# Second MoE, round two: h w2 in seven products of quarters, weights kept in DRAM, outputs added by transfers

## The chip, the cores and the metric

One core of a Trainium2 chip. The metric is the device time of one execution in microseconds, lower is better; the times are those of whole executions, the trace is of one profiled execution.

## The reference

Attention in chunks, a gated MoE, and a second MoE; the change concerns the last.

```python
def _moe2_ref(x, domain_probs, w1, w2):      # x: 1536 tokens x 512
    p = domain_probs / (domain_probs.sum(-1, keepdims=True) + 1e-09)
    out = np.zeros((N, D), dtype=np.float32)
    for e in range(E):                        # 4 experts, 1024 features each
        h = np.maximum(x @ w1[e], 0.0)
        out += p[:, e:e + 1] * (h @ w2[e])
    return out
```

## The kernel before

Every float32 operand of a matmul is held as a high part (rounded to fp32r) and a low part (the rest), and one product is three matmuls: high by high, high by low, low by high (mm3, lines 176 to 179). All of TensorE's matmuls of the second MoE come from these three lines.

The order of instructions is written out by hand: each engine takes its instructions in the order in which the program emits them, and each waits for the buffers that it reads or overwrites. SyncE (SP) issues all transfers of the second MoE, in program order as well. A pool's tile waits until the readers of the tile before it in the same buffer are done.

The second MoE (second_block, line 359) runs in two rounds of 768 tokens, and each round in 8 blocks; a block is one expert's half of the features (512), as two groups of rows. Blocks are counted through: 0 to 7 in round one, 8 to 15 in round two.

The first layer of a block, x w1, is done by Winograd's form of Strassen's method: seven products of quarters for eight (tokens in halves of HT = 384, input features in halves, output features in halves). unit(n, u) (line 405) does them for one half u of the output columns: product(n, u, m) (line 375) is 6 matmuls of 384 columns into a PSUM tile b, e or a. In between, held (line 400, ScalarE) copies a partial sum out of PSUM, and the next product is added onto the same PSUM tile, so that product has to wait for the copy. total (line 395, VectorE) adds up, h_hi (line 387, ScalarE) and h_lo (line 390, VectorE) apply relu and split. In a block: products 1, 7, then the left-over of the block before (prev), products 6, 2, 4, 5, and product 3 later.

The second layer, h w2, is plain: o_part (line 443) does, for one tile of 128 tokens and one half u, 6 matmuls of 512 columns; 12 such parts make a block (72 matmuls), one of them being carried into the next block as prev. flush (line 452, VectorE) adds the scaled result into acc; in the last block of a round acc is sent out.

The weights of block n+1 are prepared while block n runs. w1_prep (line 236, 9 steps) makes the seven quarter sums of w1 and splits them: 7 casts on ScalarE, 7 subtractions and 4 sums on VectorE. w2_prep (line 272, 5 steps) splits w2: 4 casts, 4 subtractions. Raw weights come by raw1_to (4 buffers, two per group) and raw2_to (2 buffers, both of one group). The steps are put in a list, hooks; hook() takes one step off at a place in the matmul order: two places in each o_part, while at least two steps stay in the list, and the rest in the units of the next block. y_prep_late does the same for the tokens of round two. PSUM has 8 banks for these tiles, taken in turn.

Of the kernel before, what the change touches and what calls it, by code (L numbers as in the profile page):

```python
# [42 lines left out]
RT = 2 * HT // 128  # L43
NGR = 2
GW = FE // 2 // NGR

# [22 lines left out]
def fused_kernel(ctx: ExitStack, tc: tile.TileContext, kq0, kq1, kvw, kvc, vl, w_g, w_v, w_o, w_1, w_2, probs, out):  # L69
# [23 lines left out]
    def f32(ap):  # L93
        return ap.bitcast(F32)
# [98 lines left out]
    blocks = [(0, e, g) for e in range(NE) for g in range(NGR)]  # L193
    blocks += [(1, e, g) for e in reversed(range(NE)) for g in reversed(range(NGR))]

    groups = [b[1:] for b in blocks[:NE * NGR]] + [b[1:] for b in blocks[NE * NGR + 1:]]
    group_of = [n if n < NE * NGR else n - 1 for n in range(len(blocks))]
    yr, yops, raw1, raw2s = [], [], {}, {}
    ops1, ops2 = {}, {}
    pools = {}  # L200

    def raw1_to(n):
# [25 lines left out]
    def both(*parts):  # L228
        return lambda: [p() for p in parts]
# [6 lines left out]
    def w1_prep(n):  # L236

        t = {}

        def start():  # L240
            raw1_to(n + 1)
            r0, r1 = raw1[n]
            t.update(a11=r0[:, :2], a12=r0[:, 2:], a21=r1[:, :2], a22=r1[:, 2:])
            ops1[n] = {}

        def hi(m, a):
            def do():
                w = wp.tile([128, 2, 2, GW], F32R, tag="w", name=f"w1_{n}_{m}")
                ops1[n][m] = w
                nc.scalar.copy(out=w[:, 0], in_=t[a])  # L250
            return do

        def lo(m, a):
            def do():
                w = ops1[n][m]
                nc.vector.tensor_tensor(out=w[:, 1], in0=t[a], in1=f32(w[:, 0]), op=ALU.subtract)  # L256
            return do

        def comb(dst, a, b, op):
# [12 lines left out]
    def w2_prep(n):  # L272
        def hi(u, fh):
            def do():
                raw2_to(n + 1)
                w = pools["wp2"].tile([128, 2, DM], F32R, tag="w2", name=f"w2_{n}_{u}_{fh}")
                ops2[n, u, fh] = w
                nc.scalar.copy(out=w[:, 0], in_=raw2s[n][fh][:, u])  # L278
            return do

        def lo(u, fh):
            def do():
                w = ops2[n, u, fh]
                nc.vector.tensor_tensor(out=w[:, 1], in0=raw2s[n][fh][:, u], in1=f32(w[:, 0]), op=ALU.subtract)  # L284
                if (u, fh) == (1, 1):
                    raw2_to(n + 2)
            return do


        h, l = ([fn(u, fh) for u in range(2) for fh in range(2)] for fn in (hi, lo))  # L290
        return [both(h[0], h[1], l[0]), both(h[2], l[1]), l[2], h[3], l[3]]

    def y_ops():

# [60 lines left out]
    def emit(todo, n):  # L355
        for _ in range(min(n, len(todo))):
            todo.pop(0)()

    def second_block():
        sp = ctx.enter_context(tc.tile_pool(name="sp", bufs=1, reuse_waits="tile"))  # L360
        wp2 = pools["wp2"] = ctx.enter_context(tc.tile_pool(name="wp2", bufs=7, reuse_waits="tile"))
# [4 lines left out]
        H2, hooks = {}, []  # L366
        raw2_to(1)

        def hook(n=1, keep=0):
# [3 lines left out]
            return sp.tile([128, HT], F32, tag=name, bufs=n, name=name)  # L373

        def product(n, u, m, ps, first):
            w, y = ops1[group_of[n]][m], yops[0][m]
# [28 lines left out]
        def unit(n, u, prev):  # L405

            b, e = ps_tile(f"b{n}_{u}"), ps_tile(f"e{n}_{u}")
            product(n, u, 1, b, True)
            s1 = held(b)
            product(n, u, 7, e, True)  # L410
            s7 = held(e)
            a = None
            if prev is None:
                a = ps_tile(f"a{n}_{u}")
# [12 lines left out]
            c21 = total("v", e, s2)  # L427
            h_lo(n, u, (0, 0), c11)
            h_hi(n, u, (1, 0), c21)
            product(n, u, 5, b, False)  # L430
            c22 = total("v", b, s7)
            h_lo(n, u, (1, 0), c21)
            h_hi(n, u, (1, 1), c22)
            h_lo(n, u, (1, 1), c22)
            hook()

            def finish():
                product(n, u, 3, b, False)
# [4 lines left out]
        def o_part(n, d, tt, u, first, last, cols):  # L443
            th, c = divmod(tt, RT // 2)
            c = slice(c * 128, (c + 1) * 128)
            for fh in range(2):
                h, w = H2[n, u, (fh, th)], ops2[group_of[n], u, fh]
                mm3(d[:, cols], h[:, 0, c], h[:, 1, c], w[:, 0, cols], w[:, 1, cols],
                    first and fh == 0, last and fh == 1)
                hook(keep=2)  # L450

        def flush(n, d, tt, cols):
            j, e, g = blocks[n]
            i = n - j * NE * NGR
            p, a = p_sb[:, j * RT + tt, e:e + 1], acc[tt][:, cols]
            if i == 0:
# [3 lines left out]
            if i == NE * NGR - 1:  # L460
                t0 = (j * RT + tt) * 128
                nc.sync.dma_start(out=out[t0:t0 + 128, cols], in_=a)

        ALL = slice(0, DM)
        prev = None
        hooks.extend(w2_prep(0))
        for n in range(len(blocks)):
            end = n == len(blocks) - 1
            if n == 2:
                for do in y_sums(1, yr[0], nc.vector)[2].values():  # L470
                    do()
# [2 lines left out]
                hook(2)  # L474
            fin1 = unit(n, 1, fin0)
            hook(len(hooks))

            if n == NE * NGR - 1:
                hooks.extend(y_prep_late(1))
            elif not end:  # L480
                g = group_of[n + 1]
                hooks.extend(w1_prep(g) + w2_prep(g))
            ds, waiting = {}, []

            def part(tt, u, d_first=0, d_last=1):
                if tt not in ds:
# [18 lines left out]
            part(4, 0)  # L505
            flushed(3)
            part(4, 1)
            if not end:
                part(5, 0)
                flushed(4)  # L510

                def prev(n=n, ds=ds):
                    o_part(n, ds[5], 5, 1, False, True, ALL)
                    flush(n, ds[5], 5, ALL)
            else:
                flushed(4)
                for c0 in range(0, DM, DM // 2):
                    cols = slice(c0, c0 + DM // 2)
                    d = ps_tile(f"d{n}_5_{c0}")
                    for u in range(2):  # L520
                        o_part(n, d, 5, u, u == 0, u == 1, cols)
                    flush(n, d, 5, cols)
        pools["yo"].release()


# [430 lines left out]
```

## Time and profile before

| | us |
|---|---|
| median of 3 runs | 850.06 (849.72 to 851.29) |
| the profiled execution | 849.83 |
| its span, first to last instruction | 848.1 |
| round one, first matmul of block 0 to first of block 8 | 344.57 to 593.34 |
| round two, to the start of the last matmul | 593.34 to 844.63 |

PE is TensorE's matmuls, PEld its weight loads, DVE VectorE, ACT ScalarE, POOL GpSimd, SPq the queue of SyncE that issues transfers. A matmul's record is longer than the spacing to the next, since they overlap; spacing is read from the starts.

### The profile page before, as it was taken

Reading aid. Unit: us, or ns where it says so; the run is one execution under the profiler, and the core shown is the slowest. Engines: PE = TensorE matmul, PEld = TensorE weight load, DVE = VectorE, ACT = ScalarE, POOL = GpSimd, SP = SyncE. Lnnn points to the kernel's source line nnn. Section 1 sums busy time; section 2 is a strip of 40 time slices with the busy share of each in tenths; the row PEclk is TensorE's granted clock in tenths of the full one; section 3 lists DMA queues with packets and bytes.
Section 4 is the critical chain, followed back from the end, with each engine's and each line's share of the span. In section 5 each row is a group of like instructions: output and inputs, shape, how many; then the busy total and the mean of one; then the engine's idle time right before and its main releaser. Section 6 shows DMA issues by size and latency. Waiting matters only on the chain.

```text
span 848.1 us, 11989 instructions
## 1 busy us (share of the span) xinstructions
PE 841.7 (99%) x4826; PEld 744.0 (88%) x4826; DVE 485.4 (57%) x863; ACT 350.8 (41%) x726; POOL 19.9 (2%) x23
## 2 busy tenths in 40 slices
PE   9999999999999999999999999999999999999998
PEld 6899998888888888889988988988998998998997
DVE  7854346432342239468668567565667657657753
ACT  5765354332232345435334334433434533524520
POOL 2311000000000000000000000000000000000000
PEclk9999999999999999999999999999999999999999
DMA  8974134121120000322122122022022022020001
GB/s 305 370 277 160 28 124 147 50 73 40 63 75 1 1 0 18 131 77 65 59 75 91 34 75 99 26 75 75 26 76 99 26 84 91 26 100 25 26 1 75
DMA packets 18647, 69.23 MB, mean 82 GB/s; under 512 B 2320, under 2 KB 2592, under 8 KB 18592
## 3 DMA queue, kind: packets, MB, share of 16 engines
q1 hardware_dynamic: 18560, 68.45, 23.1%
q8 instruction: 38, 0.62, 0.3%
q14 instruction: 17, 0.14, 0.1%
q0 software_dynamic: 32, 0.02, 0.0%
HBM read 65.31 MB, written 3.15 MB: 81 GB/s over the span
## 4 chain that ended last, share of the span: by engine, by line
PE 97%; ACT 1%; DVE 1%; DMA 0%; POOL 0%; issue 0%; ACTq 0%; DVEq 0%
PE d L179 10%; PE d L178 10%; PE d L177 10%; PE b L178 5%; PE b L177 5%; PE b L179 5%; PE pv L177 4%; PE pv L179 4%; PE pv L178 4%; PE pg L177 4%; PE pb L179 4%; PE pb L177 4%; PE pg L178 4%; PE pg L179 4%; PE pb L178 4%; PE e L177 3%
## 5 line engine op out<-in xcount | busy, mean ns | idle before, releaser
L459 DVE SCALAR_TENSOR_TENSOR acc<-d,p_sb,acc 128x512 f32<-128x512 f32 (+1 forms) x85 | 59.9, 741 | 75.3 <-PE d L179 75.3
L402 ACT COPY s<-b 128x384 f32<-128x384 f32 x64 | 30.4, 475 | 169.5 <-PE b L179 169.5
L177 PE MATMUL b<-yo,w 128*128 128x384 f32 x256 | 86.5, 338 | 0.7 <-ACT s L402 0.7
L178 PE MATMUL b<-yo,w 128*128 128x384 f32 x256 | 86.5, 338 | 0.5 <-DVE yo L223 0.5
L179 PE MATMUL b<-yo,w 128*128 128x384 f32 x256 | 86.4, 337 | 0.0
L256 DVE TENSOR_TENSOR w<-raw,w 128x512 fp32r<-128x512 f32 x105 | 68.3, 685 | 0.0
L177 PE MATMUL pv<-xs,w_v 128*128 128x384 f32 (+1 forms) x176 | 64.2, 365 | 0.0
L250 ACT CAST w<-raw 128x512 fp32r<-128x512 f32 x105 | 60.5, 617 | 5.8 <-DVE raw L260 3.3
L179 PE MATMUL pv<-xs,w_v 128*128 128x384 f32 (+1 forms) x176 | 61.8, 351 | 0.3 <-POOL w_v L157 0.3
L178 PE MATMUL pv<-xs,w_v 128*128 128x384 f32 (+1 forms) x176 | 61.5, 349 | 0.0
L698 ACT ACTIVATE sg<-pg 128x512 f32<-128x512 f32 x36 | 21.5, 598 | 84.2 <-PE pg L179 84.2
L179 PE MATMUL pg<-xs,w_g 128*128 128x512 f32 x144 | 56.0, 389 | 0.0
L178 PE MATMUL pg<-xs,w_g 128*128 128x512 f32 x144 | 56.0, 389 | 0.0
L177 PE MATMUL pb<-hl,w_o 128*128 128x512 f32 x144 | 56.0, 389 | 0.0
L178 PE MATMUL pb<-hl,w_o 128*128 128x512 f32 x144 | 56.0, 389 | 0.0
L179 PE MATMUL pb<-hl,w_o 128*128 128x512 f32 x144 | 56.0, 389 | 0.0
L177 PE MATMUL pg<-xs,w_g 128*128 128x512 f32 x144 | 56.0, 389 | 0.0
L116 DVE TENSOR_TENSOR hl<-g,hl 128x512 fp32r<-128x512 f32 x36 | 24.7, 690 | 48.5 <-ACT hl L115 48.5
L177 PEld LDWEIGHTS b<-yo,w 128*128 128x128 f32 x256 | 48.1, 188 | 3.0 <-ACT s L402 1.0
L178 PEld LDWEIGHTS b<-yo,w 128*128 128x128 f32 x256 | 48.1, 188 | 2.8 <-DVE yo L223 0.8
L179 PEld LDWEIGHTS b<-yo,w 128*128 128x128 f32 x256 | 48.1, 188 | 0.0
L284 DVE TENSOR_TENSOR w<-raw,w 128x512 fp32r<-128x512 f32 x60 | 38.7, 685 | 12.5 <-ACT w L278 12.5
(1115 smaller groups left out, 1927.4 us busy)
## 6 DMA issues: line engine op xcount, KB each, us to landing
raw<-in_w_dram SPq DMA_DIRECT2D x60, 512.0 KB, 3.8
kv<-in_kvc_dram SPq DMA_DIRECT2D x20, 483.0 KB, 6.5
raw<-in_w_v_dram SPq DMA_DIRECT2D x12, 512.0 KB, 6.7
raw<-in_w_g_dram SPq DMA_DIRECT2D x12, 512.0 KB, 5.1
raw<-in_w_o_dram SPq DMA_DIRECT2D x12, 512.0 KB, 3.4
kv<-in_kvw_dram SPq DMA_DIRECT2D x8, 395.0 KB, 4.7
out_dram<-acc SPq DMA_DIRECT2D x11, 256.0 KB, 2.0
kv<-in_vl_dram SPq DMA_DIRECT2D x4, 195.0 KB, 3.1
```

The costliest lines, as they stand in the source:

```text
L116: nc.vector.tensor_tensor(out=lo, in0=src, in1=f32(hi), op=ALU.subtract)
L177: nc.tensor.matmul(out=ps, lhsT=w_hi, rhs=r_hi, start=first, stop=False, skip_group_check=more)
L178: nc.tensor.matmul(out=ps, lhsT=w_hi, rhs=r_lo, start=False, stop=False, skip_group_check=more)
L179: nc.tensor.matmul(out=ps, lhsT=w_lo, rhs=r_hi, start=False, stop=last, skip_group_check=more)
L250: nc.scalar.copy(out=w[:, 0], in_=t[a])
L256: nc.vector.tensor_tensor(out=w[:, 1], in0=t[a], in1=f32(w[:, 0]), op=ALU.subtract)
L284: nc.vector.tensor_tensor(out=w[:, 1], in0=raw2s[n][fh][:, u], in1=f32(w[:, 0]), op=ALU.subtract)
L402: nc.scalar.copy(out=s, in_=ps[:, :HT])
L459: nc.vector.scalar_tensor_tensor(out=a, in0=d[:, cols], scalar=p, in1=a, op0=ALU.mult, op1=ALU.add)
L698: nc.scalar.activation(out=sg, in_=ps, func=AF.Sigmoid)
```

## The change

Round one (blocks 0 to 7) keeps its matmuls. New there: w2_sums makes the four further quarter operands of w2 that seven products need (4 sums and 4 subtractions on VectorE, 4 casts on ScalarE, 6 steps), in place in the raw tiles, taken off a list thooks in the units of the same block (for block 0: in hooks, between w1_prep(1) and w2_prep(1)). raw2_to for the next group, which stood at the end of w2_prep, now stands at the end of w2_sums. For groups 0 to 6 every prepared operand of w1 and w2, high and low, is stored to DRAM (kept1, kept2: 14 operands of 512 KB per group) by SP as soon as its subtraction is issued. Group 7 stays on the chip and serves block 8.

Round two (blocks 8 to 15) is a function of its own, round_2. It loads the prepared operands instead of raw weights (load_w1, load_w3) and prepares nothing. h is split by token halves and feature halves; four sums of its quarters per u (s_sum, VectorE) and their split give seven left operands. q does one product for a tile of 128 tokens: per u three matmuls of 256 columns. The first layer's products of u = 1 and the q products are interleaved, and the q products of the third token tile and of product 3 are carried into the next block (left). Results: ScalarE copies a partial sum, scaled by p, into a staging tile (stage), further products are added onto the same PSUM tile, and VectorE adds that to the staged part (second). From block 9 on, the sum goes from the staging tile to acc by an accumulating transfer issued on POOL; in block 8 it is written to acc directly, and in block 15 the last parts are added by VectorE, behind which SP sends acc out as whole tiles of 256 KB.

The diff, cut to its core:

```diff
--- before.py
+++ after.py
 ...
@@ -193,10 +197,13 @@
     blocks = [(0, e, g) for e in range(NE) for g in range(NGR)]
     blocks += [(1, e, g) for e in reversed(range(NE)) for g in reversed(range(NGR))]
 ...
+    kept = ctx.enter_context(tc.tile_pool(name="kept", bufs=1, space=bass.MemoryType.DRAM))
+    kept1 = [kept.tile([128, 7, 2 * 2 * GW], F32, name=f"kept1_{g}") for g in range(NSP)]
+    kept2 = [kept.tile([128, 7, 2, 2, DH], F32, name=f"kept2_{g}") for g in range(NSP)]
     yr, yops, raw1, raw2s = [], [], {}, {}
-    ops1, ops2 = {}, {}
+    ops1, ops2, ops3 = {}, {}, {}
     pools = {}
 ...
@@ -254,6 +261,8 @@
             def do():
                 w = ops1[n][m]
                 nc.vector.tensor_tensor(out=w[:, 1], in0=t[a], in1=f32(w[:, 0]), op=ALU.subtract)
+                if n < NSP:
+                    nc.sync.dma_start(out=kept1[n][:, m - 1], in_=f32(w.rearrange("p l k f -> p (l k f)")))
             return do
 
         def comb(dst, a, b, op):
@@ -282,13 +291,44 @@
             def do():
                 w = ops2[n, u, fh]
                 nc.vector.tensor_tensor(out=w[:, 1], in0=raw2s[n][fh][:, u], in1=f32(w[:, 0]), op=ALU.subtract)
-                if (u, fh) == (1, 1):
-                    raw2_to(n + 2)
+                if n < NSP:
+                    for d in range(2) if fh else range(1):
+                        nc.sync.dma_start(
+                            out=kept2[n][:, d + 1 if fh else 0, u], in_=f32(w[:, :, d * DH:(d + 1) * DH]))
             return do
 
 
         h, l = ([fn(u, fh) for u in range(2) for fh in range(2)] for fn in (hi, lo))
         return [both(h[0], h[1], l[0]), both(h[2], l[1]), l[2], h[3], l[3]]
+
+    def w2_sums(n):
+
+        r0, r1 = raw2s[n]
+        b = dict(b11=r0[:, :, :DH], b12=r0[:, :, DH:], b21=r1[:, :, :DH], b22=r1[:, :, DH:])
+        ops3[n] = {}
+
+        def comb(dst, x, y, op):
+            return lambda: nc.vector.tensor_tensor(out=b[dst], in0=b[x], in1=b[y], op=op)
+
+        def hi(m, x):
+            def do():
+                w = ops3[n][m] = wp.tile([128, 2, 2, DH], F32R, tag="w", name=f"w3_{n}_{m}")
+                nc.scalar.copy(out=w[:, :, 0], in_=b[x])
+            return do
+
+        def lo(m, x):
+            def do():
+                w = ops3[n][m]
+                nc.vector.tensor_tensor(out=w[:, :, 1], in0=b[x], in1=f32(w[:, :, 0]), op=ALU.subtract)
+                if n < NSP:
+                    nc.sync.dma_start(out=kept2[n][:, m - 1], in_=f32(w))
+            return do
+
+        return [
+            comb("b11", "b12", "b11", ALU.subtract), both(hi(5, "b11"), comb("b12", "b22", "b12", ALU.subtract)),
+            both(lo(5, "b11"), hi(7, "b12"), comb("b22", "b11", "b22", ALU.subtract)),
+            both(lo(7, "b12"), hi(6, "b22"), comb("b21", "b21", "b22", ALU.add)),
+            both(lo(6, "b22"), hi(4, "b21")), both(lo(4, "b21"), lambda: raw2_to(n + 2))]
 
     def y_ops():
 
@@ -356,6 +396,319 @@
+    def round_2(prev, hook, hooks, hp, sp, acc, held, product):
 ...
+        def load_w1(n, k):
+            if n <= ends:
+                m = M_USE[k]
+                w = ops1.setdefault(n, {})[m] = wp.tile([128, 2, 2, GW], F32R, tag="w", name=f"w1_{n}_{m}")
+                nc.sync.dma_start(
+                    out=f32(w.rearrange("p l k f -> p (l k f)")), in_=kept1[2 * NR1 - 1 - n][:, m - 1])
+
+        def load_w3(n, k):
+            if n <= ends:
 ...
+                nc.sync.dma_start(out=f32(w), in_=kept2[2 * NR1 - 1 - n][:, m - 1])
+
 ...
+        def s_sum(n, u, m):
+            c11, c21, c22, r21 = C[n, u]
 ...
+        def q(n, m, ps, tt, us=(0, 1), first=False):
+            c = slice(tt * 128, (tt + 1) * 128)
+            for u in us:
+                h, w = HO[n, u, m], w3_of(n, m, u)
+                mm3(ps[:, :DH], h[:, 0, c], h[:, 1, c], w[0], w[1], first and u == 0, u == 1, not first)
+
 ...
+        def stage(n, th, tt, dh, ps):
+            p, a, _ = of(n, th, tt, dh)
+            if n == ends and (th, dh) == (1, 1):
+                nc.vector.scalar_tensor_tensor(out=a, in0=ps[:, :DH], scalar=p, in1=a, op0=ALU.mult, op1=ALU.add)
+                return
+            st = firsts[th, tt, dh] = next_of("st", staged)
+            nc.scalar.activation(out=st, in_=ps[:, :DH], func=AF.Copy, scale=p)
+
+        def second(n, th, tt, dh, ps):
+            p, a, t = of(n, th, tt, dh)
+            if n == ends and (th, dh) == (1, 1):
+                nc.vector.scalar_tensor_tensor(out=a, in0=ps[:, :DH], scalar=p, in1=a, op0=ALU.mult, op1=ALU.add)
+                nc.sync.dma_start(out=out[(RT + t) * 128:(RT + t + 1) * 128], in_=acc[t])
+                return
+            st = firsts.pop((th, tt, dh))
+            to = a if n == NR1 else st
+            nc.vector.scalar_tensor_tensor(out=to, in0=ps[:, :DH], scalar=p, in1=st, op0=ALU.mult, op1=ALU.add)
+            if n > NR1:
+                nc.gpsimd.dma_start(out=a, in_=st, accum_op=ALU.add)
+
 ...
+        for n in range(NR1, len(blocks)):
 ...
+            b = ps_tile(f"b{n}_0")
+            product(n, 0, 1, b, True)
+            s1 = held(b)
+            if late:
+                do("3_0")
+                do("3_1")
+                E2 = ps_tile(f"E2_{n}")
+            e = ps_tile(f"e{n}_0")
+            product(n, 0, 7, e, True)
+            s7 = held(e)
+            if late:
+                left["7"](E2)
+                load_w3(n, 4)
+            else:
+                prev()
+            product(n, 0, 6, b, False)
+            s2 = held(b)
 ...
+            for k in range(5 if late else 1):
+                load_w1(n + 1, k)
+
+            b0, b = b, ps_tile(f"b{n}_1")
+            product(n, 1, 1, b, True)
+            nc.scalar.activation(out=r21, in_=b0[:, :HT], func=AF.Relu)
+            s1 = held(b)
 ...
+            q(n, 1, B[0], 0, (0,), True)
+            product(n, 1, 6, b, False)
 ...
+            q(n, 1, B[1], 1, (0,), True)
+            product(n, 1, 3, b, False)
+            for k in range(5 if late else 1, 7):
+                load_w1(n + 1, k)
 ...
+            for tt in range(2):
+                q(n, 1, B[tt], tt, (1,), True)
+                stage(n, 0, tt, 0, B[tt])
 ...
+            for tt in range(2):
+                q(n, 2, A[tt], tt, first=True)
+                second(n, 0, tt, 0, A[tt])
 ...
+            q(n, 1, B[2], 2, first=True)
+            stage(n, 0, 2, 0, B[2])
+            q(n, 2, A[2], 2, first=True)
+            for k in range(4):
+                load_w3(n + 1, k)
 ...
+            for u in range(2):
+                for tt in tts:
+                    q(n, 7, E[tt], tt, (u,), True)
+            for tt in tts:
+                stage(n, 1, tt, 1, E[tt])
 ...
+            for u in range(2):
+                for tt in tts:
+                    q(n, 6, B[tt], tt, (u,))
+            for tt in tts:
+                stage(n, 1, tt, 0, B[tt])
 ...
+            for tt in tts:
+                q(n, 4, E[tt], tt)
+                second(n, 1, tt, 0, E[tt])
 ...
+            for tt in tts:
+                q(n, 5, B[tt], tt)
+                second(n, 1, tt, 1, B[tt])
 ...
@@ -407,8 +760,14 @@
             b, e = ps_tile(f"b{n}_{u}"), ps_tile(f"e{n}_{u}")
             product(n, u, 1, b, True)
             s1 = held(b)
+            if u == 0 and n:
+                hook(len(hooks))
+                thooks.extend(w2_sums(n))
+            if u:
+                emit(thooks, 1)
             product(n, u, 7, e, True)
             s7 = held(e)
+            emit(thooks, 1)
             a = None
             if prev is None:
                 a = ps_tile(f"a{n}_{u}")
@@ -427,12 +786,15 @@
             c21 = total("v", e, s2)
             h_lo(n, u, (0, 0), c11)
             h_hi(n, u, (1, 0), c21)
+            if u == 0:
+                emit(thooks, 1)
             product(n, u, 5, b, False)
             c22 = total("v", b, s7)
             h_lo(n, u, (1, 0), c21)
             h_hi(n, u, (1, 1), c22)
             h_lo(n, u, (1, 1), c22)
             hook()
+            emit(thooks, 1)
 
             def finish():
                 product(n, u, 3, b, False)
 ...
@@ -474,13 +832,16 @@
                 hook(2)
             fin1 = unit(n, 1, fin0)
             hook(len(hooks))
-
-            if n == NE * NGR - 1:
+            emit(thooks, len(thooks))
+
+            if n == NR1 - 1:
                 hooks.extend(y_prep_late(1))
-            elif not end:
-                g = group_of[n + 1]
-                hooks.extend(w1_prep(g) + w2_prep(g))
-            ds, waiting = {}, []
+            else:
+                hooks.extend(w1_prep(n + 1))
+                if n == 0:
+                    hooks.extend(w2_sums(0))
+                hooks.extend(w2_prep(n + 1))
+            ds = {}
 
 ...
+        round_2(prev, hook, hooks, hp, sp, acc, held, product)
         pools["yo"].release()
```

## Rows read from the trace of the kernel before

**Rows 1.** the page: busy time, granted clock by slices, the chain by engine

```profile
PE 841.7 (99%) x4826; PEld 744.0 (88%) x4826; DVE 485.4 (57%) x863; ACT 350.8 (41%) x726; POOL 19.9 (2%) x23
...
PEclk9999999999999999999999999999999999999999
...
PE 97%; ACT 1%; DVE 1%; DMA 0%; POOL 0%; issue 0%; ACTq 0%; DVEq 0%
```

**Rows 2.** stretches: length, busy us of each engine, clock, DMA share, GB/s

```profile
718.65:749.80 31.15, 31.15 (x158) 28.22 (x156) 20.77 (x35) 12.92 (x25) 0.00 (x0) 1.00 0.18 68
```

**Rows 3.** who waited for whom, TensorE: total us, times, longest

```profile
PE b L177 <- ACT s L402: 0.7, 1, 0.7
```

**Rows 4.** order of time, TensorE, one block: start, us, engine, line, operation

```profile
718.65 0.33 PE L177 MATMUL b<-yo,w 128*128 128x384 f32 x1
...
719.72 0.33 PE L177 MATMUL e<-yo,w 128*128 128x384 f32 x1
...
720.58 0.33 PE L179 MATMUL e<-yo,w 128*128 128x384 f32 x1
...
728.44 0.34 PE L177 MATMUL b<-yo,w 128*128 128x384 f32 x1
...
729.32 0.34 PE L179 MATMUL b<-yo,w 128*128 128x384 f32 x1
...
733.70 0.39 PE L177 MATMUL d<-w,h_(0, 0)_6532 128*128 128x512 f32 x1
...
734.17 0.40 PE L179 MATMUL d<-w,h_(0, 0)_6532 128*128 128x512 f32 x1
...
749.80 0.33 PE L177 MATMUL b<-yo,w 128*128 128x384 f32 x1
```

**Rows 5.** order of time, TensorE, the last tile, in halves of 256 columns

```profile
843.07 0.28 PE L178 MATMUL d<-w,h_(1, 1)_7417 128*128 128x256 f32 x1
...
844.63 0.28 PE L179 MATMUL d<-w,h_(1, 1)_7417 128*128 128x256 f32 x1
```

**Rows 6.** groups by shape, from 820 us: busy us, mean ns

```profile
L459 DVE SCALAR_TENSOR_TENSOR acc<-d,p_sb,acc 128x256 f32<-128x256 f32 x2 | 1.0, 484 | 1.6 <-PE d L179 1.6
L402 ACT COPY s<-b 128x384 f32<-128x384 f32 x2 | 0.9, 470 | 0.5 <-PE b L179 0.5
```

**Rows 7.** table by stretches, three stretches with a full transfer queue

```profile
25.00:30.00 5.00, 5.00 (x70) 4.30 (x69) 4.40 (x11) 4.18 (x13) 1.28 (x1) 1.00 1.01 401
...
370.00:374.00 4.00, 4.00 (x20) 3.30 (x19) 3.13 (x5) 0.00 (x0) 0.00 (x0) 1.00 0.88 342
401.00:405.00 4.00, 4.00 (x19) 3.31 (x18) 3.28 (x6) 0.00 (x0) 0.00 (x0) 1.00 0.92 355
```

**Rows 8.** order of time, VectorE, block 0, around w1_prep(1)

```profile
361.14 0.69 DVE L256 TENSOR_TENSOR w<-raw,w 128x512 fp32r<-128x512 f32 x1
...
366.20 2.49 DVE L256 TENSOR_TENSOR w<-raw,w 128x512 fp32r<-128x512 f32 x4
```

**Rows 9.** order of time, SyncE queue: loads of raw w2 of group 1

```profile
355.27 1.93 SPq L216 DMA_DIRECT2D raw<-in_w_dram  x2
```

**Rows 10.** order of time: casts of w2_prep(1), product 6 of block 1

```profile
366.38 1.66 ACT L278 CAST w<-raw 128x512 fp32r<-128x512 f32 x3
...
378.81 0.33 PE L177 MATMUL b<-yo,w 128*128 128x384 f32 x1
```

**Rows 11.** the page, transfers: count, KB each, us to landing

```profile
raw<-in_w_dram SPq DMA_DIRECT2D x60, 512.0 KB, 3.8
...
out_dram<-acc SPq DMA_DIRECT2D x11, 256.0 KB, 2.0
...
p_in<-in_probs_dram POOLq DMA_DIRECT2D x1, 24.0 KB, 4.8
```

**Rows 12.** table by stretches, behind the last matmul

```profile
845.00:846.00 1.00, 0.00 (x0) 0.00 (x0) 0.43 (x1) 0.00 (x0) 0.00 (x0) 1.00 0.26 90
...
847.00:847.50 0.50, 0.00 (x0) 0.00 (x0) 0.00 (x0) 0.00 (x0) 0.00 (x0) 0.50 0.00 0
```

More of the change, by code (lines that the diff above doesn't have):

```diff
@@ L45 @@
 GW = FE // 2 // NGR
+DH = DM // 2
+NSP = NE * NGR - 1
+M_USE = (1, 7, 6, 2, 5, 4, 3)
+Q_USE = (1, 2, 7, 6, 4, 5, 3)
 VW = NG * NC * (D + 1)
@@ L194, in fused_kernel @@
     blocks += [(1, e, g) for e in reversed(range(NE)) for g in reversed(range(NGR))]
-    groups = [b[1:] for b in blocks[:NE * NGR]] + [b[1:] for b in blocks[NE * NGR + 1:]]
-    group_of = [n if n < NE * NGR else n - 1 for n in range(len(blocks))]
+    NR1 = NE * NGR
+    groups = [b[1:] for b in blocks[:NR1]]
+    kept = ctx.enter_context(tc.tile_pool(name="kept", bufs=1, space=bass.MemoryType.DRAM))
+    kept1 = [kept.tile([128, 7, 2 * 2 * GW], F32, name=f"kept1_{g}") for g in range(NSP)]
+    kept2 = [kept.tile([128, 7, 2, 2, DH], F32, name=f"kept2_{g}") for g in range(NSP)]
     yr, yops, raw1, raw2s = [], [], {}, {}
-    ops1, ops2 = {}, {}
+    ops1, ops2, ops3 = {}, {}, {}
     pools = {}
@@ L365, in second_block @@
         acc = [accp.tile([128, DM], F32, name=f"acc{t}") for t in range(RT)]
-        H2, hooks = {}, []
+        H2, hooks, thooks = {}, [], []
         raw2_to(1)
@@ L375, in product @@
         def product(n, u, m, ps, first):
-            w, y = ops1[group_of[n]][m], yops[0][m]
+            w, y = ops1[NR1 - 1 if n == NR1 else n][m], yops[0][m]
             fc = slice(u * 128, (u + 1) * 128)
@@ L446, in o_part @@
             for fh in range(2):
-                h, w = H2[n, u, (fh, th)], ops2[group_of[n], u, fh]
+                h, w = H2[n, u, (fh, th)], ops2[n, u, fh]
                 mm3(d[:, cols], h[:, 0, c], h[:, 1, c], w[:, 0, cols], w[:, 1, cols],
@@ L452, in flush @@
         def flush(n, d, tt, cols):
[L453 to L456, printed above, removed]
+            p, a = p_sb[:, tt, blocks[n][1]:blocks[n][1] + 1], acc[tt][:, cols]
+            if n == 0:
                 nc.vector.tensor_scalar(out=a, in0=d[:, cols], scalar1=p, scalar2=None, op0=ALU.mult)
@@ L459, in flush @@
                 nc.vector.scalar_tensor_tensor(out=a, in0=d[:, cols], scalar=p, in1=a, op0=ALU.mult, op1=ALU.add)
-            if i == NE * NGR - 1:
-                t0 = (j * RT + tt) * 128
-                nc.sync.dma_start(out=out[t0:t0 + 128, cols], in_=a)
+            if n == NR1 - 1:
+                nc.sync.dma_start(out=out[tt * 128:(tt + 1) * 128, cols], in_=a)
         ALL = slice(0, DM)
@@ L466, in second_block @@
         hooks.extend(w2_prep(0))
-        for n in range(len(blocks)):
-            end = n == len(blocks) - 1
+        for n in range(NR1):
             if n == 2:
@@ L476, in second_block @@
             hook(len(hooks))
-            if n == NE * NGR - 1:
+            emit(thooks, len(thooks))
+            if n == NR1 - 1:
                 hooks.extend(y_prep_late(1))
-            elif not end:
-                g = group_of[n + 1]
-                hooks.extend(w1_prep(g) + w2_prep(g))
-            ds, waiting = {}, []
+            else:
+                hooks.extend(w1_prep(n + 1))
+                if n == 0:
+                    hooks.extend(w2_sums(0))
+                hooks.extend(w2_prep(n + 1))
+            ds = {}
             def part(tt, u, d_first=0, d_last=1):
@@ L507, in second_block, with prev @@
             part(4, 1)
[L508 to L522, printed above, removed]
+            part(5, 0)
+            flushed(4)
+            def prev(n=n, ds=ds):
+                o_part(n, ds[5], 5, 1, False, True, ALL)
+                flush(n, ds[5], 5, ALL)
+        round_2(prev, hook, hooks, hp, sp, acc, held, product)
         pools["yo"].release()
```

188 lines of the change are left out of this document (added).

## The prediction

> **What bounds the kernel now.** I read the page first. TensorE is busy in 99% of the span, its granted clock is at the top in every slice, and 97% of the chain that ended last is its own work [rows 1]. So the time is the number of matmuls times their spacing, plus whatever makes TensorE wait. Second, the table of stretches for one block of the second MoE: in 31.15 us VectorE works 20.77 us and ScalarE 12.92 us [rows 2], so both have room, as averages. Third, the list of who waited for whom: over both rounds the longest wait of TensorE is one of 0.7 us, for a ScalarE copy [rows 3]. A bare matmul stream, then: fewer or shorter matmuls pay at once, and every new wait costs its full length. Fourth, the order of time on TensorE, to get the spacings; last, the SyncE queue and the transfers around block 0, since the change puts 7 x 7.34 = 51 MB into DRAM and takes them out again.
>
> **Part 1, the products of quarters in round two.** A block runs from 718.65 to 749.80, 31.15 us [rows 4]. Five spacings of a 384-column matmul take 0.86 us in one product and 0.88 in another [rows 4]: 0.172 and 0.176, and I take 0.174. The 84 of them in a block make 14.6 us and stay. The rest, 16.5 us, is the 72 matmuls of 512 columns, 0.229 each; two spacings in the slower stretch behind the products take 0.47, 0.235 each [rows 4]. The change replaces them by 7 products x 3 token tiles x 2 x 3 = 126 matmuls of 256 columns. The last tile of the kernel already runs such matmuls: 13 spacings take 1.56 us, 0.120 each [rows 5]. 126 x 0.120 = 15.1 us, a gain of 1.4 per block. If the slower kind shows up here too, about 5 ns each, it is 126 x 0.125 = 15.75 and the gain 0.75. I take 0.122: 15.35 us, block 29.95, gain 1.15 to 1.2, and over the 8 blocks of round two 9.3 us (bounds 6 and 11.2). One eighth of the columns is saved (32,256 for 36,864), but 54 more matmuls per block give a good part back. The first of the eight blocks keeps the small waits it has now.
>
> [...]
>
> Does round two keep TensorE fed? Per later block ScalarE gets 6 copies out of PSUM at 0.47 [rows 6], 16 relus and casts of 384 columns at about 0.5, and 12 scaled copies of 256 columns, under 0.47: at most 17 us of 30. VectorE gets 6 sums and 22 high/low or quarter sums of 384 columns at about 0.55, and 9 additions of 256 columns at 0.484 [rows 6]: 20 us of 30, as now. The preparation of w1 and w2 (7 + 4 casts, 11 + 4 subtractions and sums) is gone. Written out in order, the operand that is tightest is the low part of h for product 6, second half: relu after product 3, two sums, cast, subtraction, ready some 0.4 us before its matmul. I cost it at nothing; if each of the seven later blocks lost those 0.4 us again, 3 us. Weights: 14 transfers of 0.524 MB per block are 7.34 MB, 245 GB/s, where the queue has carried 342 to 401 [rows 7]; each is issued 15 to 25 us before its use. Bounds 0 and the second rival.
>
> **Part 2, the work added to round one.** VectorE gets 4 sums and 4 subtractions more per block, 8 x 0.61 (four in a row take 2.49 with 0.685 for the last [rows 8]) = 4.9 us: 20.8 becomes 25.7 of 31.1, hidden, but with small reserve; ScalarE 4 casts, 2.2 us, hidden. Stores of 7.34 MB and loads of 2.1 MB per block make 303 GB/s, 85% of what the queue carries; a store keeps buffers, and these come round a block later. I put 0.5 us (0 to 3) on all of this.
>
> **Part 3, the wait that I expect, in block 1.** The raw w2 of a group lies in two buffers, and there are only two, so group 1 can be loaded only when group 0 has been read. Now that is after w2_prep(0): its transfers go out at 355.27 and the second right behind [rows 9], and ScalarE casts them from 366.38 [rows 10], 11 us later. After the change the same buffers are read until the end of w2_sums(0), which stands in the list of steps behind all nine of w1_prep(1), and the load stands behind its last subtraction. VectorE works through w1_prep(1) from 361.14 to 368.7 [rows 8]; then 8 operations x 0.61 and two additions into acc x 0.66: 374.9. Only then is the load of group 1 issued, 20 us later than now, and on SP it stands behind 7 stores of w1, 2 loads of raw w1 and 4 stores of w2 sums: 13 x 0.524 = 6.8 MB, that came up from 361.8 on. At 350 GB/s [rows 7] these take 19.5 us, until about 381.5; the two loads take 3 more, and a single such transfer lands 3.8 us after issue where its bytes take 1.5 [rows 11], so both are there at about 386.5.
>
> What is queued behind that wait? Three steps of w2_prep(1) are emitted inside block 0 (22 places for steps, the last two of 20 steps kept back), and ScalarE takes its instructions in order. Its casts wait for the load, and behind them stands the copy of b after the first product of block 1. TensorE adds product 6 onto that b at 378.81 [rows 10] and may not before the copy. Three casts and the copy, 1.7 us, after 386.5: 388.3. TensorE stands still for 9.5 us. Bounds: with an empty queue the loads are there at 375 + 3.8 + 1.5 = 380.3 and the wait is 3.2 us; at 300 GB/s it is 13. I take 9.5, since two rows of a full queue lie at 342 and 355 and one at 401. VectorE stands behind the same load, with three additions into acc in its line.
>
> [...]
>
> **Part 4, the tail.** Now the last tile leaves in two halves, and from the last matmul to the end of the span it takes 848.1 - 844.75 = 3.35 us. Then six transfers of 256 KB leave in the last 5 us, in the order of SP, and the first three wait for accumulating transfers of 128 KB, issued from POOL, which has nothing else to do then, after the addition on VectorE. Such a transfer is not in the trace. The nearest rows: 2.0 us to landing for a 256 KB store, 4.8 for the one transfer from POOL [rows 11]. With 3 us the end moves by 1.5 us (0.5 to 4).
>
> **Sum.** The profiled execution took 849.83 (span 848.1 and 1.7 around it), 0.23 below the median 850.06. 849.83 - 9.3 + 0.5 + 9.5 + 1.5 + 1.5 = 853.5; against the median 853.8. I predict 853.8 us.
>
> **Rivals.** First, the gain wins: the transfers run at the 401 GB/s of the best row [rows 7], 6.8 MB are through at 379.3, both loads there at 383.4, the wait is 6.2 us, the clock costs nothing, and 256 columns take 0.120 flat: 849.83 - 11.2 + 6.2 + 0.5 = 845.3, faster. For it: that row mixes transfers as the change does. Against it: the other two rows lie at 342 and 355, and even then a wait is there. It decides below a wait of about 7 us. Second, the accumulating transfers fill the queue of round two: 12 x 0.131 MB per block, of which each is a read of the source, a read of the target and a write; if that costs three times its bytes, 7.34 + 4.7 MB need 34.4 us at 350 GB/s where TensorE needs 30. Six such blocks lack 26 us, of which the early issue of the weights hides 15 to 20: 853.5 + 8 = 861.5. Against it: the source and the target lie on the chip, and only if the price is above about 2 do 30 us not suffice. [...] Third, the two large terms cancel: a wait of 7 to 8 us with a gain of 9 to 10, 848.5 to 851.5, no change that could be measured. That 256-column matmuls might be held up by their weight loads, so that the change does not save at all, I leave out: the last tile shows them at 0.120 [rows 5].
>
> **How the numbers follow.** Forecast 0.48, its own range 852 to 858; the gain wins 0.22; the queue of round two 0.14; cancelled 0.16. About 0.2%, 1.7 us, is what a measurement of this kernel can tell from no change. Faster 0.22, within 0.16, slower 0.62. The range takes in the first rival to its centre and the second to its centre: 845.5 to 861.5.
>
> **What would show each step.** Part 1: 256-column matmuls of q at 0.119 to 0.125 apart, later blocks of round two 29.7 to 30.4 us. Part 3: in the list of waits, ScalarE's casts of w2 behind a transfer of raw w2 for some 12 us, and TensorE behind a ScalarE copy of b at block 1 for 9.5 us; group 1's load issued near 375; the granted clock below 1 for some us behind it. Part 2: blocks 2 to 7 at 31.1 to 31.3. Part 4: 4 to 6 us from the last matmul to the end. If that wait is missing or under 4 us, the forecast is wrong and the kernel is faster; if round one costs more than 15 us, or later blocks of round two grow, it is slower than the range.

## The result, and the profile after

| | kernel before | changed kernel |
|---|---|---|
| median of its runs, us | 850.67 (849.72 to 852.56, 6 runs) | 856.53 (854.76 to 857.35, 6 runs) |
| ratio to before, 95% interval | 1 | 1.0063 (1.0046 to 1.0080) |
| the profiled execution / its span, us | 849.83 / 848.1 | 854.76 / 852.5 |

The change makes the kernel slower, by 0.6%. The profiled execution of the changed kernel is the shortest of its six; what follows is read from it, and the scatter comes back with the experiments.

The page of the changed kernel, the lines that answer to [rows 1]: busy time by engine, the granted clock in 40 slices, the chain by engine, and two transfers (count, KB each, us to landing).

```profile
PE 834.3 (98%) x5246; PEld 756.7 (89%) x5246; DVE 514.4 (60%) x963; ACT 392.7 (46%) x835; POOL 88.0 (10%) x101
...
PEclk9999999999999999998999999999999999999999
...
PE 93%; DMA 2%; DVE 2%; ACT 1%; issue 0%; SPq 0%; POOL 0%; ACTq 0%; DVEq 0%
...
raw<-in_w_dram SPq DMA_DIRECT2D x32, 512.0 KB, 6.6
...
acc<-st POOLq DMA_DIRECT2D x78, 128.0 KB, 5.3
```

TensorE is busy for 7.4 us less, with 420 more matmuls, and still the span is longer. The chain names the loss: 2% of it is now DMA, and one slice of the clock, the nineteenth, is no longer full. The order of time on TensorE gives the borders of the stages (start, us, engine, line, operation; the time waited and for what in brackets):

```profile
604.74 0.33 PE L181 MATMUL b<-yo,w 128*128 128x384 f32 x1
...
613.98 0.41 PE L181 MATMUL b<-yo,w 128*128 128x384 f32 x1 [1.37 <-DVE c L453]
...
692.05 0.34 PE L181 MATMUL b<-yo,w 128*128 128x384 f32 x1
...
721.83 0.34 PE L181 MATMUL b<-yo,w 128*128 128x384 f32 x1
...
846.28 0.28 PE L183 MATMUL B<-w_raw,hx 128*128 128x256 f32 x1
```

Round one begins at 344.62 and round two at 604.74; before they began at 344.57 and 593.34. So round one takes 260.12 us for 248.77, 11.35 more. Round two, to the start of the last matmul, takes 241.54 for 251.29 (last matmul at 844.63 [rows 5]), 9.75 less. From there to the end of the span it is 6.22 us for 3.47, 2.75 more, and outside the span 2.26 for 1.73, 0.5 more. 11.35 - 9.75 + 2.75 + 0.5 + 0.05 = 4.9, which is 854.76 - 849.83.

Where round one lost it: who waited for whom (total us, times, longest), from 344 us on; then ScalarE, SyncE's queue and TensorE around block 1 in order of time.

```profile
ACT w L287 <- DMA raw<-in_w_dram: 20.4, 14, 10.6
...
PE b L181 <- ACT s L755: 9.0, 2, 8.3
```

```profile
361.90 7.90 SPq L265 DMA_DIRECT2D kept<-w  x7
369.85 2.51 SPq L215 DMA_DIRECT2D raw<-in_w_dram  x2
372.46 2.93 SPq L324 DMA_DIRECT2D kept<-w  x4
375.45 1.51 SPq L223 DMA_DIRECT2D raw<-in_w_dram  x2
...
384.46 0.62 ACT L287 CAST w<-raw 128x512 fp32r<-128x512 f32 x1 [10.58 <-DMA raw<-in_w_dram]
385.71 1.14 ACT L287 CAST w<-raw 128x512 fp32r<-128x512 f32 x2 [0.63 <-DMA raw<-in_w_dram]
386.76 0.47 ACT L755 COPY s<-b 128x384 f32<-128x384 f32 x1
...
387.28 0.69 PE L181 MATMUL b<-yo,w 128*128 128x384 f32 x1 [8.27 <-ACT s L755]
387.77 0.52 PE L182 MATMUL b<-yo,w 128*128 128x384 f32 x1
```

Group 1's raw w2 is asked for at 375.45, last of 15 transfers, where the kernel before asked at 355.27 [rows 9]. ScalarE's cast waits 10.58 us for it. The copy of b stands behind three casts, and TensorE behind the copy. The table of stretches (length; busy us of PE, PEld, DVE, ACT, POOL; granted clock; DMA share; GB/s) shows the price behind the wait, a full queue before it, and a later block of round two:

```profile
366.00:386.00 20.00, 13.01 (x60) 10.77 (x59) 9.90 (x17) 3.91 (x7) 0.00 (x0) 0.94 0.93 340
...
387.28:390.62 3.34, 3.34 (x11) 3.34 (x12) 3.34 (x6) 1.33 (x3) 0.00 (x0) 0.51 0.80 266
390.62:394.00 3.38, 3.38 (x21) 3.38 (x21) 2.50 (x6) 1.56 (x3) 0.00 (x0) 1.00 0.44 154
...
692.05:721.83 29.78, 29.78 (x213) 29.78 (x211) 18.45 (x38) 15.63 (x34) 10.17 (x13) 1.00 1.03 304
```

TensorE comes out of the wait at half clock (0.51) and issues 11 matmuls in 3.34 us where the next 3.38 us hold 21. A later block of round two takes 29.78 us for the 31.15 of [rows 2].

### The profile page after: what moved, and what is told of

Same layout as the page of the kernel before. It is cut to its first block, busy times and chain, and to the rows that moved or that the text cites. A ratio compares the mean times of both kernels' runs of the same rounds, so it can differ in the third digit from the quotient of the medians.

```text
span 852.5 us, 13705 instructions
## 1 busy us (share of the span) xinstructions
PE 834.3 (98%) x5246; PEld 756.7 (89%) x5246; DVE 514.4 (60%) x963; ACT 392.7 (46%) x835; POOL 88.0 (10%) x101
## 4 chain that ended last, share of the span: by engine, by line
PE 93%; DMA 2%; DVE 2%; ACT 1%; issue 0%; SPq 0%; POOL 0%; ACTq 0%; DVEq 0%
PE b L181 5%; PE b L182 5%; PE b L183 5%; PE d L183 5%; PE d L182 5%; PE d L181 4%; PE pv L181 4%; PE pv L183 4%; PE pv L182 4%; PE pg L183 4%; PE pg L182 4%; PE pb L182 4%; PE pb L183 4%; PE pb L181 4%; PE pg L181 4%; PE B L183 3%
## 5 line engine op out<-in xcount | busy, mean ns | idle before, releaser
L524 POOL DMA_DIRECT2D acc<-st x60 | 52.4, 970 | 687.7 <-DVE st L522 682.7
L119 ACT CAST hl<-g 128x512 fp32r<-128x512 f32 x36 | 22.2, 623 | 54.8 <-PE pb L183 54.8
L181 PE MATMUL e<-yo,w 128*128 128x384 f32 x128 | 43.2, 338 | 0.2 <-ACT st L535 0.2
L293 DVE TENSOR_TENSOR w<-raw,w 128x512 fp32r<-128x512 f32 x32 | 21.2, 687 | 36.7 <-ACT w L287 28.4
```

Source lines behind the costliest of these rows:

```text
L119: nc.scalar.copy(out=hi, in_=src)
L181: nc.tensor.matmul(out=ps, lhsT=w_hi, rhs=r_hi, start=first, stop=False, skip_group_check=more)
L524: nc.gpsimd.dma_start(out=a, in_=st, accum_op=ALU.add)
```

## The experiments

Each ratio is to the kernel before, run on the same chip, with its 95% interval. The changed kernel was not run again beside them: a difference from its 856.53 us is one between medians taken at different times, at which the kernel before took 850.67, 850.83 (experiments 1 to 4) and 850.39 (5 to 7). "Tail" is always the time from the start of the last matmul to the end of the span.

**1. The load asked for sooner.** All work stays; one group of steps changes place.

```
+                if n == 0:
+                    hooks.extend(w2_sums(0))
                 hooks.extend(w1_prep(n + 1))
-                if n == 0:
-                    hooks.extend(w2_sums(0))
                 hooks.extend(w2_prep(n + 1))
```

> One step of the changed kernel is moved: in block 0 the sums of w2 stand ahead of block 1's w1 preparation, so that the two raw w2 tiles come free, and group 1's raw w2 is asked for, some 10 us sooner than at 375.45; all the work stays. Theory (round one lost its 11.4 us to one wait for that load, 8.3 us at product 6 of block 1, and to the half clock behind it): the wait falls under 0.5 us, the granted clock stays at 1.0 in that stretch, round one ends near 595 instead of 604.7, and the kernel takes 846.5 us (845 to 848). Rival A (the 49 plus 56 stores of round one, at 303 GB/s, and VectorE's extra 5 us in each block cost the time as such): nothing moves, 855 to 857. Rival B (block 1's w1 preparation, now later, becomes the wait): half the gain, 850 to 853, with waits at products 5 and 3 of block 1.

Measured: 845.33 us (844.32 to 845.53), ratio 0.9928 (0.9916 to 0.9940), 11.2 us under the changed kernel. SyncE's queue and TensorE's waits (from 344 to 597 us) of this kernel:

```profile
364.06 3.79 SPq L324 DMA_DIRECT2D kept<-w  x4
367.90 1.92 SPq L223 DMA_DIRECT2D raw<-in_w_dram  x2
369.93 6.24 SPq L265 DMA_DIRECT2D kept<-w  x7
...
PE b L181 <- ACT s L755: 0.7, 1, 0.7
```

The load stands 7.6 us earlier and ahead of the seven stores; the 8.3 us are gone, and the 0.7 that is left was there before [rows 3]. Round one takes 250.42 us. The theory holds; rivals A and B fall.

**2. The same load, as late, with an emptier queue.** In w1_prep and w2_sums:

```
-                if n < NSP:
+                if n < NSP and n != 1:
                     nc.sync.dma_start(out=kept1[n][:, m - 1], in_=f32(w.rearrange("p l k f -> p (l k f)")))
...
-                if n < NSP:
+                if n < NSP and n:
                     nc.sync.dma_start(out=kept2[n][:, m - 1], in_=f32(w))
```

and in w2_prep as in w2_sums; round two loads a neighbour's tiles in their place, so for these two groups it computes another product, with as many bytes and matmuls.

> The changed kernel without the 14 stores that stand in SP's queue ahead of group 1's raw w2 load (7 of group 1's w1, 7 of group 0's w2, 7.3 MB); round two reads a neighbouring group's prepared tiles in their place, as many bytes, so for these two groups it computes another product. Theory as the prediction had it (issued at 375.45, the load was slow because 6.8 MB stood before it): it is still issued near 375, lands some 3 us later instead of 9 to 10, the wait at product 6 falls from 8.3 to 1 to 2.5 us, and the kernel takes 849.5 us (848 to 851). Rival (the late issue alone makes the wait, the queue hardly counts): the wait stays above 6 us, 854 to 857.

Measured: 845.96 us (845.79 to 846.10), ratio 0.9938 (0.9925 to 0.9951). SyncE's queue, the waits from 344 to 420 us, and the first matmuls of blocks 1 and 2:

```profile
373.37 2.79 SPq L223 DMA_DIRECT2D raw<-in_w_dram  x2
...
ACT w L287 <- DMA raw<-in_w_dram: 5.5, 4, 1.9
...
PE b L181 <- ACT s L755: 1.6, 3, 0.8
...
376.12 0.33 PE L181 MATMUL b<-yo,w 128*128 128x384 f32 x1
...
409.24 0.33 PE L181 MATMUL b<-yo,w 128*128 128x384 f32 x1
```

The first of the two loads is issued 2 us sooner than in the changed kernel, the second is out at 376.16 for 376.96, and TensorE's longest wait is 0.8 us for 8.3. Block 1 takes 33.12 us; in the changed kernel it takes 41.39 (375.36 to 416.75) and in experiment 1 31.37 (376.17 to 407.54). So of the 10.0 us that experiment 1 takes out of block 1, the emptier queue takes out 8.3: nearly all of that is the price of the stores that stood ahead of the load, 11 of 0.524 MB since 361.9. Some 1.8 us stay with the late issue, and rather more at the changed kernel's own times. The theory holds for the mechanism; the time lies 2 us under the expected 848 to 851. An emptier queue removes most of the loss, and so does a load that is asked for sooner and stands ahead of seven of the stores. An early issue with as many bytes ahead of it as now was not tried.

**3. TensorE kept at work in the wait.**

```
+            if (n, u) == (1, 0):
+                a = ps_tile(f"a{n}_{u}")
+                for _ in range(7):
+                    product(n, u, 1, a, True)
             product(n, u, 6, b, False)
...
```

> The changed kernel with product 1 of block 1 computed seven times more, into an unused PSUM tile, in TensorE's wait before product 6 (42 matmuls of 384 columns, 7.3 us of a wait of 8.3). Theory (the ten matmuls at 0.32 instead of 0.174 us behind the wait are the clock gate's): the wait for ScalarE stays, product 6 starts when it did, its matmuls stand 0.174 apart, and the kernel gains 1.5 us: 855.0 (854.3 to 855.7). Rival A (the slow matmuls are bound by something else, as by the arriving operands): no change, 856 to 857. Rival B (the gate held the clock down longer in most executions than in the profiled one, which is the shortest of six): the gain is 2 to 3.5 us, 853 to 854.5.

Measured: 855.38 us (854.77 to 855.50), ratio 1.0048 (1.0035 to 1.0060), 1.15 under the changed kernel. The first matmuls of product 6, and their stretch in the table:

```profile
388.68 0.44 PE L181 MATMUL b<-yo,w 128*128 128x384 f32 x1 [2.05 <-ACT s L755]
388.95 0.33 PE L182 MATMUL b<-yo,w 128*128 128x384 f32 x1
...
388.68:392.00 3.32, 3.32 (x19) 3.32 (x20) 3.32 (x6) 1.32 (x3) 0.00 (x0) 1.00 0.78 268
```

The granted clock stays at 1.00, and the same 3.3 us hold 19 matmuls instead of 11. So rival A falls: the slow matmuls were the clock's. In this execution the load came later (product 6 starts at 388.68, not 387.28), so that the spans hardly differ. The medians differ by 1.15 us, but the two ratios' intervals overlap (1.0046 to 1.0080 for the changed kernel), so that the stretch shows the effect, and the medians alone do not. Rival B, a longer stretch at half clock in most executions, asked for a gain of 2 to 3.5 us, which was not seen; but the mean granted clock is on record for every execution, 0.992 to 0.996 in the six of the changed kernel (0.995 in the profiled one), and 0.996 to 1.000 here. So in some executions of the changed kernel the level was low for longer than in its profile, and what that costs stays open. These runs lie within 0.7 us, the changed kernel's within 2.6.

**4. No adding transfers in the last block.** In stage and second:

```
-            if n == ends and (th, dh) == (1, 1):
+            if n == ends:
                 nc.vector.scalar_tensor_tensor(out=a, in0=ps[:, :DH], scalar=p, in1=a, op0=ALU.mult, op1=ALU.add)
```

> The changed kernel, in the last block alone without adding transfers: VectorE adds each output part to the sum straight from PSUM (12 additions of 128x256 at 0.48 us more on VectorE, 9 copies fewer on ScalarE). Theory (the tail is 2.75 us longer since the six output stores of 256 KB are all issued in the last 3.5 us and share 370 to 390 GB/s, their bytes and not the adding transfers): the tail stays at 6 us, 855.5 to 857. Rival, the prediction's own (the stores wait for the last adding transfers): the tail falls by 1.5 to 2.7, 853.8 to 855.

Measured: 854.01 us (852.56 to 856.43), ratio 1.0035 (1.0023 to 1.0048). It moves 6 operations from ScalarE to VectorE, fewer than the expectation says. The profiled execution has the wait of block 1 (8.3 us) and half clock as before, so the tail is read by itself: the last matmul starts at 847.68 and the span ends at 852.1. First the changed kernel (SyncE's waits from 836 us on, and its output stores), then this one, with its last three stores' times to landing (shortest, median, longest):

```profile
SPq L518 <- DMA acc<-st: 25.7, 3, 24.6
...
844.47 2.24 SPq L518 DMA_DIRECT2D out_dram<-acc  x3
846.81 1.37 SPq L532 DMA_DIRECT2D out_dram<-acc  x3
```

```profile
847.08 1.76 SPq L533 DMA_DIRECT2D out_dram<-acc  x3
...
847.68 0.28 PE L183 MATMUL B<-w_raw,hx 128*128 128x256 f32 x1
848.00 0.48 DVE L532 SCALAR_TENSOR_TENSOR acc<-B,p_sb,acc 128x256 f32<-128x256 f32 x1 [0.23 <-PE B L183]
...
DMA to landing us min/median/max: 2.5/2.5/2.5
```

In the changed kernel SyncE's first three output stores each wait for an adding transfer to land, and the other three stand behind them. Here the tail is 4.4 us for 6.2, and outside the span it is 1.84 for 2.26. My theory here, that the six bunched stores make the tail, falls as the reason for the whole; the prediction's own reason, the adding transfers ahead of them, is worth 1.8 + 0.4 us by these two executions. The same last instructions took 5.4 to 6.2 us in the changed kernel and experiments 1 to 3, so the 1.8 is good to half a microsecond or so.

**5. The output stores in halves as well.** In second, and in the same way in c12:

```
-                nc.sync.dma_start(out=out[(RT + t) * 128:(RT + t + 1) * 128], in_=acc[t])
+                nc.sync.dma_start(out=out[(RT + t) * 128:(RT + t + 1) * 128, dh * DH:(dh + 1) * DH], in_=a)
```

> As the kernel without adding transfers in the last block, and the six output stores of 256 KB in two halves of columns each: the halves that product 5 and the last product do not touch are stored when they are done, so that only 128 KB by 128 KB, 0.72 us apart, leave behind the last matmuls. Read by the tail (last matmul's start to the end of the span; 6.1 us in the changed kernel, 4.4 without the last block's adding transfers, 3.4 in the kernel before). Theory (what is left, 1.0 us, is the 1.57 MB that leave bunched): tail 3.4 to 3.7, the kernel 0.8 us under the one without the adding transfers, 852.5 to 854 with the scatter of the load's landing. Rival (what is left is the closing of the software queue that the adding transfers use): tail 4.2 to 4.6.

Measured: 853.48 us (852.43 to 854.31), ratio 1.0034 (1.0022 to 1.0046). The last matmul starts at 846.64, the span ends at 850.9: tail 4.26. The last three stores, and their times to landing:

```profile
846.03 1.77 SPq L532 DMA_DIRECT2D out_dram<-acc  x3
...
DMA to landing us min/median/max: 1.7/1.7/1.7
```

4.26 is the rival's value, but the stores do land sooner, as the theory had it: the last one is issued at 847.5 and lands at 849.2, 2.5 us after the start of the last matmul, where in experiment 4 it is issued at 848.5 and lands 3.3 after. What takes the gain back is the time from that landing to the end of the span, 1.7 us for 1.1. The tail stays 0.8 us longer than before (experiment 7 takes this up).

**6. All of it, and two places of the order.** The edits of 1 and 5, and

```
-                hook(keep=2)
+                hook(keep=2 if n < NR1 - 1 else 0)
...
             s7 = held(e)
-            emit(thooks, 1)
+            if u == 0:
+                emit(thooks, 1)
...
             s2 = held(b)
+            if u:
+                emit(thooks, 1)
```

> The early sums of w2 together with the tail of half stores, and two places of the order mended: the last two pieces of the second half's y preparation stand in block 7 and no longer ahead of block 8's first total (a wait of 1.4 us), and in u = 1 one step of the w2 sums stands behind the copy of product 6 (waits of 0.1 us in each of 7 blocks). All work stays. Theory (the four gaps are independent and lie on TensorE's path): 845.3 less 2.6 (tail) less 1.4 less 0.6 is 840.7 (839.7 to 842.5), and TensorE waits for nothing over 0.3 us from 345 us on. Rival (a gap on TensorE that is closed opens at the next engine: ScalarE's cast moved behind the copy delays the first h): 0.5 to 2 us of it come back, 842.5 to 844.

Measured: 840.20 us (839.98 to 840.39), ratio 0.9877 (0.9863 to 0.9890): 10.2 us faster than the kernel before and 16.3 than the changed one. TensorE's waits from 344 to 830 us are two; with them the borders of the stages and a block of round one in the table of stretches:

```profile
PE b L181 <- ACT s L755: 0.7, 1, 0.7
PE b L181 <- DVE c L453: 0.2, 1, 0.2
...
594.18 0.33 PE L181 MATMUL b<-yo,w 128*128 128x384 f32 x1
...
834.36 0.28 PE L183 MATMUL B<-w_raw,hx 128*128 128x256 f32 x1
...
469.59:500.74 31.15, 31.15 (x158) 28.22 (x156) 25.41 (x43) 14.94 (x29) 0.00 (x0) 1.00 0.82 306
```

Round one starts at 345.42 here and takes 248.76 us, to 0.01 what it took before the change; round two takes 240.18 for 251.29; the tail is 4.24. So the stores, VectorE's 4.6 us and ScalarE's 2.0 more per block (25.41 and 14.94 for 20.77 and 12.92 [rows 2]) cost nothing once the order is right, and round two saves 11.1 us. The theory holds; nothing comes back.

**7. No adding transfers at all,** otherwise as 6: VectorE adds every part from PSUM.

```
-            if n == ends:
+            if n > NR1:
                 nc.vector.scalar_tensor_tensor(out=a, in0=ps[:, :DH], scalar=p, in1=a, op0=ALU.mult, op1=ALU.add)
```

> The same with one part of the change undone: no adding transfers at all; VectorE adds every output part from PSUM (12 more additions of 128x256 at 0.48 us in each of six blocks, 5.8 us beside 20.8 of 30, 12 copies fewer on ScalarE). Theory (the adding transfers, 78 of 128 KB at 0.97 us of GpSimd, cost TensorE nothing before the tail, and VectorE at 26.5 of 30 us has little room left): round two is longer by 0 to 1.5 us in each block through waits for VectorE, 841 to 849. Rival (the prediction's second: the transfers take bandwidth from the prepared weights): nothing longer or 1 to 3 us shorter, 838 to 841.

Measured: 844.42 us (843.66 to 845.47), ratio 0.9929 (0.9917 to 0.9942), 4.2 us slower than 6. The same stretch of 30 us in kernel 6 and in this one, and a matmul of this one:

```profile
695.00:725.00 30.00, 30.00 (x214) 30.00 (x213) 18.43 (x37) 15.85 (x35) 10.49 (x12) 1.00 1.02 298
...
695.00:725.00 30.00, 29.76 (x209) 29.28 (x209) 23.03 (x49) 10.20 (x22) 0.00 (x0) 1.00 0.66 240
...
710.00 0.39 PE L183 MATMUL B<-w_ring,h 128*128 128x256 f32 x1 [0.24 <-DVE h L468]
```

With the adding transfers the stretch holds 214 matmuls, at a DMA share of 1.02, and TensorE waits for no load. Without them the share falls to 0.66, and nothing gains by it: the rival falls. VectorE works 4.6 us more, and at 23 of 30 us, far from full, it already hands over a low part of h late in every block (TensorE waits 0.18 to 0.24 us, once in each of six): later blocks take 30.5 us for 29.8, which over six of them is the 4.2 us. So against adding on VectorE the adding transfers pay inside the round; what they cost, they cost at the end.

Without any, the tail is 843.7 - 840.04 = 3.66 us, near the 3.47 of before, where kernels 5 and 6, with none in the last block but 72 before it, have 4.26 and 4.24. In all three the last store lands 2.5 us after the start of the last matmul; the 0.6 us lie behind that landing, where the span goes on for 1.1 us here and 1.7 in kernels 5 and 6. Kernel 4 has the same 72 adding transfers and ends 1.1 us after its last landing. So the 0.6 us are seen in one execution of each kernel, and their cause is not shown.

## Why the prediction was right, point by point

- **Slower, by a wait in block 1 (part 3): right.** Round one was to lose 9.5 + 1.5 + 0.5 = 11.5 us and lost 11.35. By the spacings of TensorE that is 8.4 us of wait, 1.6 of half clock (10 spacings, 8 of them 0.32 instead of 0.174) and 1.3 of small waits; that the sum came out so near is in part luck, since the wait was put 1.1 too long and the small waits 0.8 too short. The issue was put at 374.9 and came at 375.45; the queue was put at 350 GB/s and carried 340. Only the wait is shorter than forecast, 8.3 us for 9.5: the first of the two loads let its cast start at 384.46 and the second at 385.71, where both were put at 386.5. That it is mostly the full queue is shown by experiment 2; what the late issue adds, about 2 us, is the difference between experiments 2 and 1.
- **The half clock: right in size.** The first + 1.5 of the sum stands for it, the author's estimate; no run of the kernel before shows that term, since the rows have the lower clock only behind the last matmul [rows 12]. In its place the 387 to 390.6 stretch of the changed kernel shows 1.6 us, and experiment 3 gives 1.15 between medians, not clear of noise. The rise is there as well: 0.51 up to 390.62 and 1.00 from there, with TensorE at work without a gap from 387.28 on.
- **Hidden work in round one (part 2): right as a bound.** 0.5 us (0 to 3) were put down; 1.3 were lost, and not to the engines' load. In each of blocks 1 to 7 ScalarE copied b 0.1 us too late, because a cast stood ahead of it, and that widened two spacings by 0.1 each. Experiment 6 moved the cast and round one was back at 248.76.
- **Seven products of quarters (part 1): the sum right, two terms off.** The 256-column matmuls stand 0.1195 apart on average over 942 spacings, nearer to the 0.120 of [rows 5] than to the 0.122 taken; so a block gains 31.15 - 29.78 = 1.37 us instead of 1.2, and the round 11.1 (experiment 6), just under the upper bound. Against that, "the first of the eight blocks keeps the small waits it has now" was wrong: in block 8 VectorE's first total stands behind the last two pieces of the y preparation, the second of which waits for ScalarE, and TensorE waits 1.37 us. Net 9.75 for 9.3.
- **The tail (part 4): mechanism right, the term too small.** 1.5 us (0.5 to 4) were taken; it was 2.75, and 0.5 outside the span, of which the adding transfers of the last block make about 2.2 (experiment 4, where the list of SyncE's waits shows the first three stores behind them, as forecast). The estimate of 3 us to landing was near the last ones (2.8 us) and far from the median, 5.3.
- **The rivals.** The second, a full queue in round two, is refuted: later blocks take 29.78 us beside a DMA share of 1.03 (one of them 30.21, with a wait for a ScalarE copy), no wait for a load is in TensorE's list, and taking the transfers away made the kernel slower (experiment 7). The first needed a wait below 7 us and the gain at its upper bound; the gain came near it (9.75 of 11.2), the wait was not short. The third had its two terms almost right, a wait of 8.4 us and a gain of 9.75; what makes the kernel slower all the same are the half clock, the small waits, the tail and the time outside the span, 1.6 + 1.3 + 2.75 + 0.5 = 6.2 us, which it leaves out.
- **Forecast and median.** The steps gave 853.5 for a profiled execution, which took 854.76. The median lies 1.8 above that. Where that scatter comes from stays open. With the wait the runs lie within 2.6 us, 3.9 (experiment 4) and 1.9 (5), but within 0.7 where TensorE was kept at work in it (3); without the wait they lie within 1.2, 0.4 and 1.8 (1, 6 and 7), and the kernel before lies within 2.8.

## What to carry to other kernels

A buffer that is read longer than before delays the next load into it (here the request went from 355.27 to 375.45 us): look up where that load now stands in its queue, how many bytes are ahead of it (here they were 8.3 of 10.0 us), and which engine, taking its instructions in order, will wait for it with other work behind (here ScalarE, 10.58 us, with the copy behind it that TensorE waited 8.27 for). When a change with a sound gain comes out slower, look for the one wait first; here moving one group of steps turned +0.6% into -0.7%, and two more moved steps and a repaired tail into -1.2%. Work handed to adding transfers was good in the middle of this kernel (4.2 us slower without it, experiment 7) and expensive in front of its last stores (about 2.2 us, experiment 4).

## What the hardware showed that was not expected

- In the changed kernel an adding transfer of 128 KB between buffers of the chip kept GpSimd for 0.97 us (52.4 us for 60, their mean 970 ns). It landed 5.3 us after issue in the median of all 78, where a block such as 692.05 to 721.83 has a DMA share of 1.03, but after 2.8 us in the median of the last five, from 836 us on, where the share was 0.30 from 840.00 to 844.47.
- A hold-up of TensorE of 0.1 us, too short for the list of waits, cost about 0.2 at 430.84 in the changed kernel: the next spacing, to 431.11, was widened by another 0.1 (0.28 and 0.27 for 0.174).
- With adding transfers in the last block the time outside the span was 2.19 to 2.30 us in all 20 executions (changed kernel, experiments 1 to 3), without them 1.73 to 1.86 in all 22 (experiments 4 to 7).
